# Attention and expert kernel: queries and keys with four tokens to a lane, ten output tiles, and a new order

## The chip, the cores and the metric

The kernel runs on one core of one Trainium2 chip. The metric is the time of one execution on the device, in microseconds (us). A core has five engines that run side by side: TensorE (PE), VectorE (DVE), ScalarE (ACT), GpSimd (POOL) and SyncE (SP), which here only issues transfers; 16 DMA engines move the data between the memory of the chip (HBM) and the 128 lanes of the core's own memory (SBUF). PE writes into PSUM, which has eight banks of 2 KB per lane.

## The reference

Two layers of attention, one behind the other, on 4 sequences of 768 tokens.

```python
# layer 1: q, k, v are (4, 8, 768, 64) in float32; n_global = 8, n_local = 96
scores = scale * np.matmul(q, k.transpose(0, 1, 3, 2))
is_global = pos[None, :] < int(n_global)
is_local = (rel >= 0) & (rel < int(n_local))
keep = is_global | is_local
...
a = np.exp(scores)
a = a / (np.sum(a, axis=-1, keepdims=True) + 1e-09)
x = np.matmul(a, v)
# layer 2: 4 experts of head size 64 on x as (4, 768, 512); the best 2 of 4 by x @ w_gate
for e in range(E):
    q = x @ wq[e]
    k = x @ wk[e]
    v = x @ wv[e]
    scores = scale * (q @ k.transpose(0, 2, 1))
    ...
    ye = a @ v @ wo[e]
```

In layer 1 a token sees the 8 first tokens of its sequence and the 96 last ones before it, with a bias that falls with the distance at a slope of its head's own. In layer 2 it sees all tokens before it. The output is (4, 768, 512) in float32, the weighted sum of the two best experts.

## The kernel before

**Units.** The work is cut into 24 units of 128 tokens, six to a sequence. A unit u runs through a fixed set of steps, each with a short name, and each step is a few instructions on one engine:

- `ldq`, `ldk`, `ldv` load q, k and v (SP). `cq`, `ck`, `cv` cast them to 16 bits (POOL; in the first unit ACT and DVE). `tq` and `tk` transpose on PE, `eq` and `ek` copy the result out of PSUM into qT and kT (DVE).
- `s0` and `s1` are the scores of the heads 0 to 3 and 4 to 7 (PE, line 650), `x0` and `x1` their exponentials (ACT, line 654), `m0` and `m1` the product with the mask and bias table M (DVE, line 659), `z` the product with v (PE, lines 670 and 672), `r` and `n` the division by the sum (DVE, lines 678 and 679).
- `kp` and `vp` put the 8 global tokens' keys and values over the first 8 places of a unit's k and v once that unit has used its own, so that the next unit finds them beside the local ones: `kp` is a copy on POOL, and `vp` (line 686) a transfer of 8 KB from one place of SBUF to another, issued by SP when `z` of its unit is done; `z` of the next unit waits for it. `kg` and `vg` keep the 8 tokens of each sequence in KG and VG.
- `tx` and `ex` transpose the result of layer 1; `pq` (line 704) and `pv` (line 710) are the projections of layer 2, `eqk` and `ev` take them out of PSUM, `xr`, `mx`, `wr`, `zi` make the experts' weights; `s2`, `x2` (line 746), `af` (line 754), `y2` (line 766), `rz`, `cw`, `n2` are the second attention, over all units of the sequence so far.
- `tz`, `ez`, `po` (line 789), `eo` and `so` (line 798) are the output projection, its copy out of PSUM and the store of 256 KB.

**Order.** All of this is written out by hand in one table, `ORDER`: every entry is a step and a unit (`s0-2`), with a star where the second of two allowed engines takes it, and the PSUM banks it uses behind a colon. `+14` behind the bank puts 14 idle matmuls of a zero tile ahead of the step (line 381, "busy"). Every engine, and SP, works through its own steps in the order of the table. The table starts with constants: `M-0-0` to `M-1-1` build the mask table on ACT, `w-q`, `w-k`, `w-v`, `w-o` cast the weights, `warm` is 24 idle matmuls.

**Tiles of q and k.** Before the change, units go in pairs: a block is 256 tokens of all 8 heads, one load for q and one for k, 512 KB each. A lane holds two neighbouring tokens, so a packet is 2 x 64 x 4 = 512 B. There are twelve blocks and three buffers of each kind (`RB = 3`). The transposed columns of a unit then stand in the order (token parity, lane); the mask table is built in that order, and `perm` puts it right in `tx`. `ek` is one copy of 128x1024 16-bit elements, since for k the two tokens of a lane are transposed as one 32-bit word, which leaves the keys in their own order.

**Other buffers.** Most tiles have four copies (`R = 4`), the output tile o_sb among them: `eo` of a unit waits for `so` of the unit four before it.

Of the kernel before, what the change touches and what calls it, by code (L numbers as in the profile page):

```python
# [16 lines left out]
P = 128  # L17
# [5 lines left out]
V1one* ldk-0 nil iota warm:1 ld-g ident ldk-2 perm dg ldq-0 ck0-0 ldv-0 ones d mask ident32 ldq-2 d0  # L23
d1 ck1-2 w-g M-1-0 ck1-0 ck0-2 ld-k M-0-1 tk-2:4+10 tk-0:3 cq0-0 ek-0 ldq-4 cq1-0 cv-0 M-0-0 ek-2
tq-0:6+16 vg-0 M-1-1 eq-0 ldv-1 s0-0:45+14 s1-0:67 cq0-2 x1-0 kg-0 x0-0 cq1-2 kp-0 ld-q m0-0
s1-1:01+25 m1-0 s0-1:23 x1-1 w-k* tq-2:6 z-0:45 x0-1 m1-1 vp-0 eq-2 cq0-4 r-0 kp-1 cq1-4 n-0 ldk-4
tq-4:2+19 V2one cv-1 s0-2:45 eq-4 s1-2:01 kp-2 x1-2 m0-1 ldv-2 ld-v w-q* z-1:23+10 x0-2 s1-3:01 r-1
s0-3:67 m1-2 vp-1 tx-0:5 x0-3 n-1 ck0-4 ex-0 x1-3 tx-1:2 kp-3 pq-0:6 ck1-4 ex-1 ldq-6 m0-2 pq-1:1
eqk-0* cv-2 m1-3 tk-4:7 ldv-3 eqk-1* ldk-6 w-v* z-2:45 ek-4 s20-0:01 s1-4:67 x20-0 m0-3 pv-0:3 vp-2
x1-4 r-2 af-0 s0-4:01 n-2 kp-4 x0-4 cq1-6 s0-5:67 s20-1:45 cq0-6 ldk-8 x0-5 tx-2:1 m0-4 tq-6:2 cv-3  # L30
ex-2 xr-0 x20-1 s1-5:67 m0-5 pq-2:0 ldv-4 mx-0 x1-5 wr-0 ck1-6 eq-6 z-3:45 ck0-6 vp-3 pv-2:6 r-3
zi-0 n-3 tk-6:1 xr-2 eqk-2* ldq-8 m1-4 ev-2 s20-2:45 ck0-8 ev-0* pv-1:7 x20-2 ek-6 tx-3:3 ck1-8
ldv-6 mx-2 s0-6:01 ldq-10 wr-2 cv-4 s1-6:45 ex-3 tk-8:6 x1-6 m1-5 z-4:23 ev-1 af-1 x0-6 ek-8 pv-3:5
vp-4 xr-1 af-2 r-4 s21-2:01 mx-1 xr-3 zi-2 pq-3:6 n-4 x21-2 cq0-8 mx-3 wr-1 kg-6 m1-6 ld-o y2-0:7
eqk-3* y2-1:0 kp-6 m0-6 tx-4:1 ev-3 cv-6 wr-3 s1-7:23 ex-4 s0-7:45 x1-7 cq1-8 rz-0 rz-1 y2-2:6 cw-0
vg-6 zi-1 tq-8:1 n2-0 ldv-5 x0-7 cw-1 pq-4:2 ldk-10 cq1-10 eq-8 kp-7 rz-2 tz-0:7 m1-7 eqk-4*
s21-3:45 cw-2 x21-3 ez-0 ldq-12 s20-3:23 n2-2 w-o* n2-1 tz-2:1 z-6:67 x20-3 ez-2 vp-6 r-6 s0-8:01
n-6 x0-8 cv-5 s1-8:23 s20-4:45 m0-7 po-0:7 x1-8 po-2:0 cq0-10 eo-0* tz-1:6 ldk-12 kp-8 x20-4 ez-1
z-5:23 ck0-10 eo-2* tx-6:6 ck1-10 po-1:7 ex-6 s1-9:01 r-5 eo-1 m1-8 pq-6:6 ldv-7 x1-9 n-5 cq0-12
ldk-14 s0-9:45 m0-8 eqk-6* s21-4:23 tq-10:0 kp-9 x21-4 m1-9 tx-5:6 ldv-8 tk-10:1 cq1-12 ex-5 x0-9  # L40
af-3 s20-6:23 ek-10 tq-12:7 ck1-12 pq-5:6 x20-6 ldq-14 eq-10 ck0-12 eq-12 s22-4:01 eqk-5* s1-10:23
cv-7 tk-12:7 x22-4 m0-9 z-7:45 x1-10 ek-12 ck1-14 s21-5:01 vp-7 r-7 x21-5 kg-12 pv-4:2 n-7 ck0-14
ldk-16 pv-6:3 cv-8 s0-10:45 xr-6 mx-6 xr-4 mx-4 ev-4 zi-3 tx-7:1 kp-10 x0-10 y2-3:7 ex-7 tk-14:6
m1-10 ldv-9 ev-6 s20-5:45 ldq-18 cq0-14 wr-4 s1-11:01 rz-3 x20-5 pq-7:2 cw-3 af-4 n2-3 ek-14 cq1-14
tz-3:7 z-8:45 eqk-7* wr-6 ez-3 tq-14:3 x1-11 ck0-16 vp-8 zi-4 r-8 n-8 s0-12:67 af-6 pv-7:2 x0-12
ldq-16 eq-14 ck1-16 s1-12:01 s0-11:45 x1-12 s22-5:67 m1-11 tk-16:3 ev-7 xr-7 x0-11 cv-9 y2-4:0 mx-7
wr-7 ek-16 so-1 af-5 pv-5:1 so-0 zi-6 tx-8:4 m0-10 ev-5 z-9:23 xr-5 x22-5 cq1-18 ex-8 po-3:5 r-9
kp-12 pv-8:4 n-9 cq0-18 eo-3 so-2 s0-13:67 mx-5 rz-4 cq1-16 s1-13:23 wr-5 x0-13 pq-8:5 cw-4 ldv-10
cq0-16 zi-5 n2-4 m0-11 x1-13 vp-9 tq-16:0 m1-12 tq-18:1 eqk-8* eq-16 tz-4:7 ldk-18 s20-7:23 ez-4
tx-9:5 m0-12 x20-7 y2-5:6 eq-18 ldv-12 y2-6:7 xr-8 mx-8 ev-8 ex-9 s21-8:01 s20-8:23 cv-10 ldv-11  # L50
rz-6 x21-8 rz-5 pq-9:5 wr-8 cw-6 kp-13 x20-8 n2-6 cw-5 z-10:01 zi-7 m1-13 eqk-9* po-4:7 vp-10 af-8
r-10 n2-5 s20-9:23 eo-4 n-10 s0-14:45 af-7 pv-9:6 x20-9 ck1-18 ldk-20 tz-5:0 tx-10:7 y2-8:1 ez-5
xr-9 cv-12 x0-14 zi-8 mx-9 y2-7:0 ex-10 s21-9:23 rz-8 ev-9* ldv-13 pq-10:7 cw-8 x21-9 rz-7 m0-14
so-4 cv-11 pv-10:5 n2-8 eqk-10* tz-6:4 cw-7 wr-9 s1-14:23 xr-10 ev-10 mx-10 ez-6 z-11:67 kp-14 x1-14
n2-7 ck0-18 ldv-14 wr-10 s21-10:01 zi-10 s20-10:45 vg-12 r-11 x21-10 n-11 tk-18:3 ldq-20 po-6:2
ek-18 x20-10 cv-13 po-5:7 eo-6* tz-8:6 ck0-20 z-12:01 eo-5 tx-11:3 vp-12 ez-8 s0-15:45 af-9 ex-11
s1-15:67 x0-15 r-12 zi-9 pq-11:3 af-10 ldq-22 n-12 kp-15 x1-15 m0-15 tx-12:4 y2-9:2 ex-12 eqk-11*
s0-16:01 rz-9 m0-13 s1-16:45 so-5 x0-16 s22-10:67 pq-12:3 so-3 cq0-20 cw-9 x22-10 cq1-20 n2-9
z-13:01 eqk-12* m0-16 tz-7:2 tq-20:6 x1-16 ldk-22 r-13 ez-7 n-13 cq0-22 s20-12:23 vp-13 x20-12
s20-11:45 eq-20 ck1-20 s21-11:01 tx-13:2 m1-14 x21-11 po-8:3 ldv-16 cv-14 tz-9:7 po-7:6 eo-8* x20-11  # L60
kp-16 s22-11:01 cq1-22 ez-9 tk-20:3 ex-13 x22-11 m1-16 s1-17:45 ldv-15 tq-22:7 ek-20 so-8 ck0-22
eo-7 z-14:01 x1-17 m1-15 s0-17:23 vp-14 pq-13:6 kg-18 eq-22 ck1-22 x0-17 r-14 m1-17 po-9:4 eqk-13*
tk-22:5 so-7 n-14 eo-9 cv-15 s1-18:67 s20-13:23 x1-18 s0-18:01 ldv-17 af-12 tx-14:4 ek-22 x0-18
z-15:67 cv-16 x20-13 ex-14 pv-11:0 vp-15 kp-18 r-15 m0-17 s0-19:45 xr-11 so-9 s1-19:23 m0-18 x0-19
pq-14:1 kp-19 n-15 af-11 x1-19 mx-11 ldv-18 m1-18 tx-15:6 af-13 wr-11 z-16:45 ex-15 eqk-14* cv-17
ev-11* s1-20:23 vp-16 r-16 s0-20:67 n-16 x1-20 y2-10:1 ldv-19 m0-19 s20-14:45 x0-20 s21-14:23 rz-10
pq-15:0 zi-11 so-6 cw-10 n2-10 x20-14 cv-18 z-17:67 m0-20 eqk-15* pv-12:5 kp-20 r-17 vg-18 n-17
x21-14 tx-16:4 cv-19 s1-21:01 ev-12 ex-16 s0-21:23 xr-12 x1-21 mx-12 af-14 z-18:67 wr-12 pq-16:4
vp-18 m1-19 x0-21 ldv-23 kp-21 r-18 y2-11:5 n-18 ldv-20 eqk-16* zi-12 s0-22:01 rz-11 s21-15:23
ldv-22 cw-11 x0-22 y2-12:4 n2-11 pv-14:7 rz-12 tx-18:6 cw-12 x21-15 tz-10:5 mx-14 n2-12 pv-13:1  # L70
ez-10 tx-17:0 ldv-21 ex-18 ev-13 s20-15:45 ex-17 s21-16:23 xr-14 xr-13 x20-15 m0-22 tz-11:6 pq-17:0
mx-13 ez-11 x21-16 wr-14 af-15 po-11:5 wr-13 eqk-17 po-10:6 cv-20 eo-11 ev-14* s22-16:01 s20-16:23
eo-10 m1-21 s1-22:45 x22-16 kp-22 so-10 z-19:67 zi-13 m1-20 x20-16 y2-13:0 vp-19 pq-18:1 r-19 cv-21
n-19 x1-22 so-11 af-16 rz-13 s21-17:23 eqk-18 s0-23:67 x21-17 pv-16:5 m0-21 tz-12:4 pv-15:1 x0-23
cw-13 ez-12 z-20:23 n2-13 mx-15 zi-14 tz-13:0 vp-20 xr-15 cv-23 r-20 ev-16 s22-17:67 n-20 ev-15
po-12:4 xr-16 cv-22 x22-17 mx-16 ez-13 tx-19:2 wr-16 y2-14:3 wr-15 eo-12 ex-19 s1-23:67 s20-17:01
rz-14 x1-23 cw-14 so-12 y2-15:2 zi-16 m0-23 z-21:45 zi-15 x20-17 n2-14 po-13:6 vp-21 m1-22 pv-18:7
eo-13 r-21 rz-15 pq-19:0 n-21 so-13 mx-18 cw-15 tx-20:1 n2-15 eqk-19* pv-19:6 xr-18 s20-18:45
s20-19:23 wr-18 x20-18 ev-19* y2-16:0 ex-20 x20-19 af-18 zi-18 z-22:45 rz-16 cw-16 pq-20:1 af-17
vp-22 mx-19 xr-19 ev-18 n2-16 r-22 af-19 wr-19 tz-14:7 n-22 tz-15:3 eqk-20* pv-17:6 ez-14 y2-19:2  # L80
zi-19 ev-17 m1-23 tx-21:1 xr-17 y2-18:4 tx-22:7 po-14:5 rz-18 mx-17 ex-21 y2-17:0 rz-19 wr-17 eo-14
cw-18 ex-22 pq-21:1 so-14 n2-18 rz-17 cw-19 ez-15 z-23:45 n2-19 eqk-21* s21-20:23 s20-20:67 r-23
# [267 lines left out]
def kernel(  # L350
# [56 lines left out]

    HP = P // 2  # L410
    ident = const.tile([P, P], FH, name="ident")
    ident32 = const.tile([P, P], F32, name="ident32")
    perm = const.tile([P, P], FH, name="perm")
# [463 lines left out]
```

## Time and profile before

| what | us |
| --- | --- |
| three runs | 145.97, 147.48, 148.12 |
| median of the runs | 147.48 |
| profiled execution, its own time | 146.46 |
| span of it, first to last instruction | 144.7 |
| mean granted TensorE clock in it | 0.991 |

The span is the stretch between the first and the last instruction of the program in the profiled execution; the execution's own time has 1.8 us more around it. The costliest groups of instructions by what they do, from the groups by line with shapes kept apart:

| step | engine | instructions | mean ns of one | busy us |
| --- | --- | --- | --- | --- |
| x0, x1 (128x1024) | ACT | 40 | 1031 | 39.9 |
| x2 (128x1024) | ACT | 36 | 1034 | 36.2 |
| m0, m1 (128x1024) | DVE | 40 | 777 | 30.9 |
| n | DVE | 24 | 688 | 16.5 |
| ck | POOL | 22 | 815 | 17.5 |
| cv | POOL | 24 | 694 | 16.6 |
| cq | POOL | 22 | 654 | 14.2 |
| eqk | ACT | 22 | 590 | 13.0 |
| ek | DVE | 12 | 685 | 8.1 |
| eq | DVE | 12 | 684 | 8.1 |
| eo | ACT / DVE | 16 / 8 | 598 / 687 | 9.4 / 5.5 |

Loads of q take 6.5 us in the median from issue to landing, of k 4.3, of v 3.4, stores 4.7. The DMA packets are 24,576 of 512 B (q and k), 24,576 of 256 B (v), and a few thousand of 1 and 2 KB (weights and stores).

How to read such rows: in a list of waits, a row is "engine line <- who ended the wait: us in total, times, longest". In the timeline a row is start, duration, engine, line, operation, output and input with shapes, count, and in brackets the idle time of that engine before it and what ended it. In the chain of waits a row is start, duration, and what the chain ran through.

### The profile page before, as it was taken

The numbers are of one execution on the slowest core, as the hardware profiler recorded it, in microseconds if no ns is written. First come the engines' busy times: TensorE is split into PE (matmuls) and PEld (weight loads), VectorE is DVE, ScalarE is ACT, GpSimd is POOL, SyncE is SP. The second block draws the span as 40 slices with busy tenths as digits, with TensorE's granted clock in tenths as the row PEclk, the third lists the DMA queues.
The fourth block names the chain that finished last, engine by engine and source line by source line (L and its number), as shares of the span: only waits on it lengthen the run. The fifth ranks groups of instructions, "written<-read, shape, count | busy, mean of one in ns | idle before, by whom it ended". The sixth has DMA issues, their size and how long they took to land.

```text
span 144.7 us, 5721 instructions
## 1 busy us (share of the span) xinstructions
PE 132.1 (91%) x2316; PEld 104.5 (72%) x2316; DVE 119.2 (82%) x375; ACT 116.1 (80%) x193; POOL 79.0 (55%) x142
## 2 busy tenths in 40 slices
PE   6999788899889999999999999999999999999960
PEld 2378667677765887869787957798969789886720
DVE  0265879699988997899889999899999989887970
ACT  3098567888698988988998999999999976699740
POOL 5258767698759898890659477666044304012300
PEclk9999999999999999999999999999999999999996
DMA  2999999986999997999599698565494120121463
GB/s 67 303 266 313 223 252 283 228 190 177 282 273 238 277 226 195 198 333 262 120 240 263 155 337 188 146 156 143 114 185 152 50 106 7 72 77 72 149 250 126
DMA packets 55726, 27.85 MB, mean 192 GB/s; under 512 B 26096, under 2 KB 52368, under 8 KB 55696
## 3 DMA queue, kind: packets, MB, share of 16 engines
q1 hardware_dynamic: 55696, 27.45, 73.0%
q8 instruction: 19, 0.31, 0.9%
q14 instruction: 11, 0.09, 0.2%
HBM read 20.98 MB, written 6.29 MB: 188 GB/s over the span
## 4 chain that ended last, share of the span: by engine, by line
PE 60%; ACT 11%; DMA 10%; DVE 7%; issue 4%; POOL 4%; SPq 0%; ACTq 0%; DVEq 0%; POOLq 0%
PE banks L704 11%; DMA V<-VG 7%; PE banks L650 6%; PE banks L710 6%; PE banks L509 5%; PE banks L742 5%; PE banks L766 5%; ACT A L654 4%; ACT A L746 4%; PE banks L789 4%; PE banks L381 4%; DMA rawqk<-in_k_dram 3%; PE banks L670 3%; PE banks L611 3%; PE banks L694 3%
## 5 line engine op out<-in xcount | busy, mean ns | idle before, releaser
L654 ACT ACTIVATE A<-banks 128x1024 f16<-128x1024 f32 (+1 forms) x48 | 44.4, 959 | 5.5 <-PE banks L650 5.2
L746 ACT ACTIVATE A<-banks 128x1024 f16<-128x1024 f32 (+1 forms) x48 | 42.9, 927 | 2.8 <-PE banks L742 2.4
L659 DVE TENSOR_TENSOR A<-A,M 128x1024 f16<-128x1024 f16 (+1 forms) x48 | 34.8, 736 | 3.4 <-ACT A L654 3.3
L754 POOL TENSOR_SCALAR_AFFINE_SELECT A<-A 128x512 f16<-128x512 f16 x24 | 16.1, 681 | 26.7 <-ACT A L746 21.9
L704 PE MATMUL banks<-xT,wqk 128*128 128x128 f16 x384 | 25.3, 219 | 0.1
L704 PEld LDWEIGHTS <-wqk 128*128 128x128 f16 x384 | 22.0, 98 | 1.8
L400 POOL CAST V<-rawv 128x512 f16<-128x512 f32 x24 | 16.6, 694 | 9.4 <-DMA rawv<-in_v_dram 7.3
L400 POOL CAST k<-rawqk 128x512 f16<-128x512 f32 x22 | 17.5, 815 | 2.7 <-DMA rawqk<-in_k_dram 2.4
L650 PE MATMUL banks<-qT,kT 64*128 64x128 f16 x352 | 16.8, 218 | 1.3 <-POOL kT L400 0.5
L400 POOL CAST q<-rawqk 128x512 f16<-128x512 f32 x22 | 14.2, 654 | 6.6 <-DMA rawqk<-in_q_dram 6.3
L742 PE MATMUL banks<-QK 64*128 64x128 f16 x336 | 16.0, 217 | 1.5 <-ACT A L654 0.6
L679 DVE TENSOR_TENSOR x<-banks,rall 128x512 f16<-128x512 f32 x24 | 16.5, 688 | 0.5
L400 ACT CAST QK<-banks 128x512 f16<-128x512 f32 x22 | 13.0, 590 | 4.1 <-PE banks L704 3.9
L742 PEld LDWEIGHTS <-QK 64*128 64x128 f16 x336 | 10.4, 94 | 6.6 <-issue 4.4
L710 PE MATMUL banks<-wvg,xT 128*128 128x264 f16 x96 | 14.5, 276 | 0.4 <-DVE xT L400 0.2
L650 PEld LDWEIGHTS <-kT 64*128 64x128 f16 x352 | 10.7, 94 | 5.5 <-issue 2.6
L670 PE MATMUL banks<-V,A 128*128 128x65 f16 x192 | 14.3, 193 | 0.3
L789 PE MATMUL banks<-wo,zT 128*128 128x512 f16 x48 | 13.7, 380 | 0.1
L766 PE MATMUL banks<-V,A 128*128 128x65 f16 x336 | 13.4, 193 | 0.0
L670 PEld LDWEIGHTS <-A 128*128 128x128 f16 x192 | 12.1, 97 | 1.4 <-issue 0.5
L672 PE MATMUL banks<-V,A 128*128 128x65 f16 x160 | 12.3, 193 | 0.3 <-DMA V<-VG 0.2
L766 PEld LDWEIGHTS <-A 128*128 128x128 f16 x336 | 11.9, 97 | 0.9
(72 smaller groups left out, 229.5 us busy)
## 6 DMA issues: line engine op xcount, KB each, us to landing
rawqk<-in_k_dram SPq DMA_DIRECT2D x12, 512.0 KB, 4.3
rawqk<-in_q_dram SPq DMA_DIRECT2D x12, 512.0 KB, 6.5
rawv<-in_v_dram SPq DMA_DIRECT2D x24, 256.0 KB, 3.4
out_dram<-o_sb SPq DMA_DIRECT2D x24, 256.0 KB, 4.7
w<-in_moe_wk_dram SPq DMA_DIRECT2D x1, 512.0 KB
w<-in_moe_wq_dram SPq DMA_DIRECT2D x1, 512.0 KB
w<-in_moe_wv_dram SPq DMA_DIRECT2D x1, 512.0 KB
wo<-in_moe_wo_dram SPq DMA_DIRECT2D x1, 512.0 KB
```

The costliest lines, as they stand in the source:

```text
L400: act.copy(o, i) if e == "ACT" else (dve if e == "DVE" else pool).tensor_copy(o, i)
L650: mm(sc[:, par, pr, prev * P:(prev + 1) * P], lhsT=share(kT, u - prev)[L, p, :], rhs=share(qT, u)[L, p, :], start=True, stop=True)
L654: act.activation(A1[(2 * u + hf) % (2 * R)][:, :, :, 0:w], T.pop(("s", u, hf))[:, :, :, 0:w], func=Exp, scale=scale1)
L659: eng[e].tensor_tensor(a, a, M[:, hf, :, :, :] if ri else M0[:, hf, :, :, :], op=Alu.mult)
L670: mm(z[:, h // 4, h % 4, :], lhsT=a[:, 0:P], rhs=V1[i][:, h, 0:DV], start=True, stop=not ri)
L679: add("n", lambda e: dve.tensor_tensor(x16[i][:, :].rearrange("p (f h d) -> p f h d", f=2, d=Dh), T.pop(("z", u))[:, :, :, 0:Dh], r1.unsqu ...
L704: mm(ps[:, j, :], lhsT=wqk[:, ko, j, :], rhs=xT[i][:, ko, :], start=(ko == 0), stop=(ko == nko - 1))
L710: mm(ps[:, :], lhsT=xT[i][:, ko, :], rhs=wvg[:, ko, :], start=(ko == 0), stop=(ko == nko - 1))
L742: mm(sc[:, par, n, :], lhsT=QK2[b % 2][L, ki, 2 + p2, :], rhs=QK2[b % 2][L, ri, p2, :], start=True, stop=True)
L746: act.activation(A2[i][:, :, 4 * ch:4 * ch + m, :], T.pop(("s2", u, ch))[:, :, 0:m, :], func=Exp, scale=scale2)
L766: mm(z[:, ex, :], lhsT=A2[i][:, ex % 2, n, :], rhs=V2[b % 2][:, ki, ex, 0:DV], start=(j == 0), stop=(j == len(mine) - 1))
L789: mm(ps[:, :], lhsT=zT[i][:, p2, :], rhs=wo[:, p2, :], start=(p2 == 0), stop=(p2 == E // 2 - 1))
```

## The change

Five things change at once.

1. A lane holds four neighbouring tokens of q and k, so a packet is 1 KB. The six units of a sequence are no longer three pairs: the first block is units 0 and 1 with all heads, and the other four units make two blocks, one with the heads 0 to 3 and one with 4 to 7. There are again twelve blocks of 512 KB for q and for k. The first block has only 64 lanes' worth of tokens (256/4), so its heads 0 to 3 are loaded into lanes 0 to 63 and its heads 4 to 7 into lanes 64 to 127, by two loads of 256 KB. The transposed tiles get five buffers (`RT = 5`). The steps are now called `ldq-6`, `cqa-6`, `cqb-6`, `tq-6` for a first block and `ldq0-8`, `cq0a-8`, `tq0-8` and so on (`0` and `1` for the halves of the heads) for the others.
2. The keys need a reordering on the way out of PSUM, so `ek` is two copies with pairs of elements as the innermost run. `kp` is two copies for the units 2 to 4 of a sequence. Mask table and `perm` go by four instead of two.
3. The output tile has ten copies instead of four.
4. In the last two units (22 and 23) `y2` is cut: `y1` takes the first eight entries as soon as their exponentials are there, `y2` the rest. The last two outputs are copied and stored in halves (`eo1`, `so1`).
5. The order table is new, with 1048 entries instead of 1042. Its idle matmuls are 90 instead of 94. `w-q` is on DVE instead of POOL; of `eqk` four instead of two are on DVE, of `ev` nine instead of eight, of `eo` five instead of eight.

```diff
-    RB = 3
-    rawqk = ring(RB, [P, 2, H, 2, Dh], F32, "rawqk")
+    RB, RT = 3, 5
+    rawqk = ring(RB, [P, 2, 8 * P], F32, "rawqk")
...
-    o_sb = ring(R, [P, Dm], F32, "o_sb")
+    RO = 10
+    o_sb = ring(RO, [P, Dm], F32, "o_sb")
...
+            def load(n, src):
+                def fn(e):
+                    for f in range(2) if hf is None else [None]:
+                        lanes, hs, toks = ((slice(0, P), slice(4 * hf, 4 * hf + 4), slice(2 * P, S)) if f is None else
+                                           (slice(f * P // 2, (f + 1) * P // 2), slice(4 * f, 4 * f + 4), slice(0, 2 * P)))
+                        nc.sync.dma_start(raw[n][lanes].rearrange("p h j d -> p h (j d)"),
+                                          src[b, hs, toks, :].rearrange("h (p j) d -> p h (j d)", j=4))
+                return fn
...
-            add("ek", lambda e: copy(e, kT[bl % RB][:, :, :, :].rearrange("l h a p -> l h (a p)"),
-                                     T.pop(("tk", u))[:, :, :].bitcast(FH)), {"DVE": 0.6}, ["tk"] + before(3))
+            def ek(e):
+                ps = T.pop(("tk" + gn, u)).bitcast(FH).rearrange("l (h t p j) -> l h p t j", h=2, t=2, j=2)
+                o = kT[nb % RT][:, :].rearrange("l (h p t j) -> l h p t j", h=2, t=2, j=2)
+                for p in range(2):
+                    copy(e, o[:, p, :, :, :], ps[:, p, :, :, :])
...
+        if ri == 0:
+            group("", 3 * b, None)
+        elif ri == 2:
+            for hf in range(2):
+                group(str(hf), 3 * b + 1 + hf, hf)
...
+        cut = 4 * (n_ch - 1) if u >= NU - 2 else 0
...
+        if cut:
+            add("y1", y2(0, cut), {"PE": 0.03 * 2 * cut}, ["af"] + [f"x2{ch}" for ch in range(n_ch - 1)] +
+                [("ev", b * n_rt + ki) for ki in range(ri)] + ["ev"], kind="b", until=[["rz", "cw", "n2"]])
+            add("y2", y2(cut, 2 * (ri + 1)), {"PE": 0.03 * 2 * (2 * (ri + 1) - cut)}, ["y1", f"x2{n_ch - 1}"])
...
+        parts = 2 if u >= NU - 2 else 1
...
+            add("so" + nm, lambda e, cs=cs: nc.sync.dma_start(out[b, rows, cs], o_sb[u % RO][:, cs]),
+                {"DMA": 0.92 if parts == 1 else 0.5}, ["eo" + nm])
```

The two tables begin like this on PE and on SP (the other engines' steps left out):

```
before, PE: warm tk-2+10 tk-0 tq-0+16 s0-0+14 s1-0 s1-1+25 s0-1 tq-2 z-0 tq-4+19 s0-2 s1-2 z-1+10 s1-3 s0-3 tx-0
after, PE:  warm tk-0 tk1-2 tq-0 s0-0+16 s1-0 s1-1+21 s0-1 tk0-2 tq0-2+15 z-0+6 tq1-2+9 tx-0 s0-2 s1-2+5 s1-3+8 s0-3 s0-4 s1-4 z-1
before, SP: ldk-0 ld-g ldk-2 ldq-0 ldv-0 ldq-2 ld-k ldq-4 ldv-1 ld-q vp-0 ldk-4 ldv-2 ld-v vp-1 ldq-6 ldv-3 ldk-6 vp-2 ldk-8 ldv-4 vp-3
after, SP:  ldk1-2 ldk-0 ldq-0 ldk0-2 ldv-0 ldq0-2 ldq1-2 ld-g ldv-1 ld-q ld-k vp-0 ld-v ldv-2 ldq-6 vp-1 ldk-6 ldv-3 ldk0-8 vp-2 ldk1-8 ldv-4 ldq0-8 vp-3
```

and end like this on PE:

```
before: s21-23 pv-22 po-16 pv-21 po-18 s20-23 s22-23 y2-21 y2-22 y2-20 po-19 tz-21 y2-23 tz-22 po-21 po-22 tz-20 tz-23 po-20 po-23 total
after:  s21-23 po-18 y2-21 po-19 po-16 y1-22 s20-23 y2-22 s22-23 tz-21 pv-23 y2-20 po-21 tz-22 y1-23 tz-20 y2-23 po-22 po-20 tz-23 po-23 total
```

## The prediction

> **What bounds the kernel now.** I read the page's busy shares and slices first, then the windows of 5 us, then the waits of ACT and DVE stage by stage, then the chain of waits and the timeline of the last 10 us.
>
> ```profile
> PE 132.1 (91%) x2316; PEld 104.5 (72%) x2316; DVE 119.2 (82%) x375; ACT 116.1 (80%) x193; POOL 79.0 (55%) x142
> DVE  0265879699988997899889999899999989887970
> DMA  2999999986999997999599698565494120121463
> 15.00:20.00 5.00, 3.71 (x72) 3.36 (x73) 4.01 (x10) 2.69 (x4) 3.30 (x6) 1.00 0.87 230
> 20.00:25.00 5.00, 4.31 (x78) 3.76 (x78) 4.20 (x7) 4.08 (x6) 4.12 (x6) 1.00 1.08 271
> 85.00:90.00 5.00, 4.88 (x78) 3.49 (x75) 4.96 (x8) 4.83 (x6) 4.15 (x7) 1.00 1.05 245
> 120.00:125.00 5.00, 5.00 (x110) 4.65 (x109) 4.43 (x22) 2.69 (x8) 1.03 (x2) 1.00 0.16 57
> ```
>
> The window rows give busy us of PE, PEld, DVE, ACT, POOL, then the granted clock (1.00: it is out of the argument), DMA share and GB/s. Three stages differ. From 45 to 110 us DVE and ACT are both near 95% (4.96 and 4.83 of 5): bound by their work, and an added DVE instruction counts almost whole. From 110 to 130 PE never pauses (5.00) while ACT falls to 2.69. In the first 45 us nobody is full, and the DMA engines are, until about 30 us.
>
> ```profile
> ACT A L654 <- PE banks L650: 4.4, 5, 2.3
> DVE A L659 <- ACT A L654: 3.3, 3, 1.7
> 19.06 1.94 ACT L654 ACTIVATE A<-banks 128x1024 f16<-128x1024 f32 x2 [2.31 <-PE banks L650]
> 26.48 2.85 ACT L654 ACTIVATE A<-banks 128x1024 f16<-128x1024 f32 x3
> 20.62 4.45 DMA V<-VG
> ```
>
> The two waits are those of 14 to 45 us: ACT loses 4.4 us waiting for scores, and DVE 3.3 us waiting for ACT. The exponentials of unit 2 start at 19.06 behind PE, which has tq-4 and 19 fillers ahead of s0-2; those of unit 4 start only at 26.48, since k of units 4 and 5 is a block of its own, issued at 16.71 behind vp-0 and landed at 21.0. The last row is from the chain: a copy of 8 KB (vp) takes 4.45 us, because it stands in the DMA queue behind loads.
>
> ```profile
> 134.09 1.62 PE L766 MATMUL banks<-V,A 128*128 128x65 f16 x48
> 134.18 1.98 ACT L746 ACTIVATE A<-banks 128x1024 f16<-128x1024 f32 x2
> 136.09 0.93 PE L766 MATMUL banks<-V,A 128*128 128x65 f16 x24
> 139.98 0.69 DVE L400 COPY o_sb<-banks 128x512 f32<-128x512 f32 x1 [0.44 <-ACT o_sb L400]
> ```
>
> The last exponential ends at 136.16; the last output copy at 140.67; its store, issued at 140.70, closes the span of 144.7. These 8.5 us are latency, not work.
>
> **Part 1: 1 KB packets and half lanes.** Bytes are unchanged; q and k go from 24,576 packets of 512 B to 12,288 of 1 KB. In the packet records 512 B take 32.1 ns and 1 KB (the weights) 55.6, so 16 engines save (24,576 x 32.1 - 12,288 x 55.6)/16 = 6.6 us of work in the whole run; only what lies before 30 us can show. Where 512 B packets run alone (5 to 8 us) 290 GB/s flow, with 1 KB about 325 (11 to 13, and 16 to 17 us). Until q of the first block 1.57 MB pass in both tables (k1-2, k-0, q-0 against k-0, k-2, q-0): 5.4 us against 4.8, -0.6 us. But k-0 and q-0 (1.05 MB) now come as two loads each on 64 lanes. No row has 64 lanes; the nearest is V<-VG on 8, whose packets of 1,056 B take 65.6 ns, 18% over the 1 KB ones: 3.2 us x 0.18 = +0.6. I take 0 for the head; ends -0.6 and, at half the rate of 1 KB, 3.2 - 0.6 = +2.6. ACT then still runs two casts of q (1.12 us) and eight factors (2.13) before x0-0, which began at 12.98, as before; the factor M-1-0, moved behind x1-0, delays x1-1 by 1.07 us at most, inside its wait for PE. SP issues eight more loads (0.4 us each): nothing waits for SP there but vp, which waits for z anyway.
>
> [...]
>
> **Part 2: blocks of four units by heads.** Unit 2 now needs k0-2, q0-2, and its second half k1-2, q1-2: 3.4 MB instead of 2.36 MB must be in, so s0-2 comes no earlier than 18.4 us. After that units 2 to 5 have all their scores without another load: PE's order reads s0-2 s1-2 s1-3 s0-3 s0-4 s1-4, and the waits of ACT between 20 and 30 us go. Of 4.4 us I take 2.0: the 2.31 before unit 2 stays, the later ones go; ends 0 and -4.4. What is late next is z, tied by vp: 1.25 MB stand between vp-0 and vp-1 in both tables, and between vp-1 and vp-2 too. The cast of wq goes from POOL (1.29 us a weight) to DVE, between m0-2 and m1-2: DVE has 3.2 us of idle time from 19 to 45 us to hide it; +0.5, ends 0 and +1.2.
>
> **Part 3: ek in two pieces.** One copy of 128x1024 f16 takes 685 ns, one of 128x512 f16 (xT) 417: 12 x (2 x 417 - 685) = +1.8 us on DVE, of which some 85% lie in full stages: +1.5. The read goes in pairs of elements, which no row shows; if it falls to the speed of an f32 copy (687 ns for 512), 12 x (2 x 687 - 685) = +8.3. Lower end +0.9 (instructions overlap by 75 ns: 0.34 from start to start). The row of xT is nearest, as PSUM, f16 and length agree.
>
> **Part 4: the table in the middle.** Two eqk, one ev more and three eo fewer on DVE: 2 x 692 + 413 - 3 x 687 = -0.3; ACT gets the reverse, +0.2. Counting PE's matmuls ahead of each pq, the tables differ by under 2 us throughout, so the solid PE stage neither moves nor shrinks: 0, ends -1 and +1. kp in two pieces adds 12 x 0.2 us to POOL, which is idle for 45% of the span. If POOL's cover fails (it has 4.85 of 5 from 30 to 35), the same 2.4 us would come in at kp, before the next unit's scores. Ten output tiles let stores wait without holding eo; the waits at eo are for po (ACT 2.7, DVE 0.6) and for ACT's eo (0.4), none for a store: 0.
>
> **Part 5: the tail.** Behind s22-23 PE has 72 matmuls of y2 (30 ns), 5 po (0.43), 4 tz (0.11) now: 4.7 us; then 36, 4, 4 and one pv (0.45): 3.7, so -1.0. The last copy in halves on ACT and DVE: 0.69 to about 0.42, -0.3. The last store lands after 4.0 us; one that ran alone took 2.0, so half the bytes give -0.7. Against it 36 matmuls of y2 and a po (1.5 us) stand ahead of s20-23 and s22-23 now; ACT was full there (133.7 to 136.2), I charge 0.5. Sum -1.5, ends 0 and -2.5.
>
> **Sum.** 0 - 2.0 + 0.5 + 1.5 - 0.3 - 1.5 = -1.8 us. The profiled execution took 146.46 (span 144.7 and 1.8 around it); the median of the runs is 147.48. From 147.0 between them: 145.2.
>
> **Rivals.**
> Paid in full: half lanes cost nothing (-0.6), ACT's regained time reaches DVE whole (-3.3, its wait), ek at the overlapped price (+1.0), the rest as above: -0.6 - 3.3 + 0.5 + 1.0 - 0.3 - 2.0 = -4.7, so 142.3. For it: the waits are there, in a stage that feeds all others. Against it: DVE is full from 45 us on and has more to do.
> Slower, by half lanes: if a half-lane load runs at half rate, k-0 and q-0 add 2.6, and k-6 and q-6, which stand ahead of vp-1 and vp-2, 1.6 each on the chain through z: 145.2 + 5.8 = 151.0. It decides from about 80 ns a packet on half lanes: (80/55.6 - 1) x 3.2 - 0.6 = 0.8 at the head and 0.7 for each of the other two, 2.2 in all, and the gain is gone. For it: vp has 4.45 us on the chain already. Against: the 65.6 ns of V<-VG.
> Slower, by ek at 8.3: 145.2 + 6.8 = 152.0. For it: DVE is full. Against: both sides stay two-byte runs.
> No effect (packets were hidden anyway, and what the tail gains is lost ahead of it): 147.0.
>
> **How the numbers follow.** Forecast 0.42 (its own range 143.8 to 146.8), paid in full 0.33, half lanes 0.16, ek 0.05, no effect 0.04. A difference under about 2% can't be told from none here; 2% under 147.48 is 144.5. Faster: 0.30 of the second and 0.08 of the first, 0.38. Slower: 0.14 + 0.05 and 0.01, 0.20. Within: 0.42. The range 142.0 to 149.2 reaches over the second case and into the third's lower sizes; under 142 I leave 0.07, above 0.13.
>
> **What would show it.** Packets: mean of 1 KB packets of q and k, apart for the first blocks, near 56 to 66 ns; from 80 up the half lanes decide. Part 2: ACT's wait for scores between 14 and 45 us at 2.4 or less, unit 4's first exponential before 24 us. Part 3: the copies of kT at 24 x 417 ns. Tail: under 7.5 us from the last exponential's end to the span's end. I am wrong if DVE's idle time before 45 us doesn't shrink, or if the middle stages, not head and tail, carry the difference.

## The result, and the profile after

The kernel after takes 152.67 us (median of 152.22, 153.11, 154.62 and 151.81), where the kernel before took 146.92 beside it: 1.037 times as long, with an interval of 1.025 to 1.049. It is slower, and outside the range of the prediction (142.0 to 149.2); nearest is its rival "slower, by half lanes" (151.0). Ratios, here and below, are to runs of the kernel before on the same chip and leave disturbed runs out, which the medians don't. The profiled execution took 152.22 us, 5.8 more than that of before, with a span of 150.4.

The page's busy times and three of its rows of 40 slices:

```profile
PE 135.5 (90%) x2312; PEld 107.4 (71%) x2312; DVE 118.5 (79%) x388; ACT 115.9 (77%) x195; POOL 79.6 (53%) x153
DVE  1143498779998938889999899979889989977960
PEclk9995999999999996999999999999999999999996
DMA  2999939999869997989939946476900141222862
```

DVE has no more work than before (118.5 against 119.2 us), so its work in sum is not what costs 5.8 us. The idle places of DVE are the first slices and slice 15 (53 to 56 us), and in the clock row two slices, 4 and 16, stand at 5 and 6 tenths; before had no such slice ahead of its end. The windows show the same (busy us of PE, PEld, DVE, ACT, POOL, then the granted clock, DMA share, GB/s):

```profile
5.00:10.00 5.00, 4.61 (x24) 2.24 (x22) 1.48 (x4) 0.12 (x1) 1.98 (x4) 1.00 1.13 222
10.00:15.00 5.00, 3.89 (x40) 3.33 (x41) 1.43 (x4) 4.05 (x12) 2.68 (x6) 0.66 1.14 314
50.00:55.00 5.00, 2.57 (x46) 1.99 (x41) 3.34 (x6) 3.88 (x4) 2.37 (x4) 1.00 1.16 209
55.00:60.00 5.00, 5.00 (x68) 4.46 (x68) 3.85 (x8) 2.33 (x4) 4.96 (x8) 0.66 0.81 230
125.00:130.00 5.00, 5.00 (x115) 4.47 (x113) 4.73 (x22) 2.72 (x6) 1.94 (x3) 1.00 0.17 59
```

From 5 to 10 and from 50 to 55 us the DMA engines are full (a share of 1.13 and 1.16) and move only 222 and 209 GB/s; from 10 to 15, just as full, 314. The slow windows are those in which loads of 64 lanes run. The solid stage of PE (125 to 130: 5.00, ACT 2.72) is the one that before had from 120 to 125, only later.

The waits between 14 and 45 us, in total, times and the longest:

```profile
ACT A L709 <- PE banks L705: 5.3, 4, 3.1
DVE kT L401 <- PE banks L649: 3.7, 1, 3.7
DVE A L714 <- ACT A L709: 0.3, 1, 0.3
```

ACT's wait for scores has grown from 4.4 to 5.3 us. DVE's wait for ACT has gone (3.3 to 0.3), but DVE now waits as long for the transposes of k0-2, which the new table puts ahead of unit 0's products. Three transfers in the chain of waits are longer than any in the chain of before, whose longest is a load of k of 5.05 us (start, us):

```profile
3.55 6.57 DMA rawqk<-in_q_dram
26.71 5.77 DMA rawqk<-in_k_dram
46.94 8.00 DMA V<-VG
```

The first is the load of q-0: ACT casts it from 10.20 us on, in the kernel before from 9.61. The second is the upper half of k-6. The third is a vp that stands behind q-12 and k-12, 8.00 us for 8 KB, where the vp in the chain of before took 4.45 and 5.04 us. The end of the span:

```profile
140.19 1.94 ACT L807 ACTIVATE A<-banks 128x1024 f16<-128x1024 f32 x2 [0.17 <-PE banks L803]
145.74 0.37 ACT L401 COPY o_sb<-banks 128x256 f32<-128x256 f32 x1 [0.85 <-PE banks L866]
146.15 0.42 DVE L401 COPY o_sb<-banks 128x256 f32<-128x256 f32 x1 [0.76 <-ACT o_sb L401]
```

From the last exponential's end (142.13) to the span's end (150.4) pass 8.3 us, before 8.5; the two halves of the last copy run one behind the other.

### The profile page after: what moved, and what is told of

Same layout as the page of the kernel before. It is cut to its first block, busy times and chain, and to the rows that moved or that the text cites. A ratio compares the mean times of both kernels' runs of the same rounds, so it can differ in the third digit from the quotient of the medians.

```text
span 150.4 us, 5766 instructions
## 1 busy us (share of the span) xinstructions
PE 135.5 (90%) x2312; PEld 107.4 (71%) x2312; DVE 118.5 (79%) x388; ACT 115.9 (77%) x195; POOL 79.6 (53%) x153
## 4 chain that ended last, share of the span: by engine, by line
PE 57%; DMA 15%; ACT 13%; DVE 5%; issue 3%; SPq 2%; POOL 2%; ACTq 0%; DVEq 0%; POOLq 0%
PE banks L765 10%; DMA V<-VG 7%; PE banks L705 6%; PE banks L836 6%; ACT A L807 6%; PE banks L803 6%; PE banks L771 6%; PE banks L866 5%; DMA rawqk<-in_q_dram 4%; DMA rawqk<-in_k_dram 4%; ACT A L709 4%; PE banks L642 3%; PE banks L725 3%; PE banks L382 3%; PE banks L649 3%; PE banks L727 3%
## 5 line engine op out<-in xcount | busy, mean ns | idle before, releaser
L815 POOL TENSOR_SCALAR_AFFINE_SELECT A<-A 128x512 f16<-128x512 f16 x24 | 16.6, 698 | 23.6 <-ACT A L807 18.3
L765 PE MATMUL banks<-xT,wqk 128*128 128x128 f16 x384 | 25.9, 221 | 0.2
L401 POOL CAST k<-rawqk 128x512 f16<-128x512 f32 x22 | 16.7, 790 | 10.0 <-DMA rawqk<-in_k_dram 10.0
L401 POOL COPY kT<-KG 128x16 f16<-128x16 f16 (+1 forms) x32 | 9.1, 298 | 19.2 <-PE banks L705 19.1
L705 PE MATMUL banks<-qT,kT 64*128 64x128 f16 x352 | 17.4, 222 | 1.4 <-ACT A L709 0.7
L401 POOL CAST V<-rawv 128x512 f16<-128x512 f32 x24 | 16.0, 667 | 4.7 <-DMA rawv<-in_v_dram 4.5
L401 ACT CAST QK<-banks 128x512 f16<-128x512 f32 x20 | 12.0, 602 | 5.3 <-PE banks L765 5.3
L725 PE MATMUL banks<-V,A 128*128 128x65 f16 x192 | 14.7, 193 | 1.5 <-POOL V L401 1.0
L725 PEld LDWEIGHTS <-A 128*128 128x128 f16 x192 | 12.2, 97 | 5.2 <-issue 3.2
L727 PE MATMUL banks<-V,A 128*128 128x65 f16 x160 | 12.3, 193 | 2.9 <-DMA V<-VG 2.8
L401 ACT COPY o_sb<-banks 128x512 f32<-128x512 f32 (+1 forms) x21 | 11.8, 574 | 3.1 <-PE banks L866 3.0
L836 PE MATMUL banks<-V,A 128*128 128x65 f16 x336 | 14.1, 193 | 0.0
```

Of the source, the lines that this page charges most:

```text
L401: act.copy(o, i) if e == "ACT" else (dve if e == "DVE" else pool).tensor_copy(o, i)
L705: mm(sc[:, par, pr, prev * P:(prev + 1) * P], lhsT=share(kT, u - prev, hf)[L, pr, :], rhs=share(qT, u, hf)[L, pr, :], start=True, stop=True)
L725: mm(z[:, h // 4, h % 4, :], lhsT=a[:, 0:P], rhs=V1[i][:, h, 0:DV], start=True, stop=not ri)
L727: mm(z[:, h // 4, h % 4, :], lhsT=a[:, P:2 * P], rhs=V1[(u - 1) % R][:, h, 0:DV], start=False, stop=True)
L765: mm(ps[:, j, :], lhsT=wqk[:, ko, j, :], rhs=xT[i][:, ko, :], start=(ko == 0), stop=(ko == nko - 1))
L836: mm(z[:, ex, :], lhsT=A2[i][:, ex % 2, n, :], rhs=V2[b % 2][:, ki, ex, 0:DV], start=(lo == 0 and n == (ex // 2 if cut else mine[0][0]) an ...
```

## The experiments

The theory after these readings: loads of 64 lanes are slow and put everything behind them off, at the start and at each sequence again. Its rivals: the order of the table (ek0-2 ahead of unit 0's products), the half clock after PE's pauses, ek in two pieces. The kernel after has a ratio of 1.037 [1.025, 1.049]; times in us per part are differences of ratios, with the interval in brackets where it matters. In the runs with odd and even lanes the line numbers are 9 to 11 higher than in the kernel after.

**Half lanes on the kernel before.**

```diff
-    rq[:, n, ...], src[b, :, ri * P:(ri + 2) * P, :]
+    for f in range(2) if ri == 0 else [None]:
+        rq[f * P // 2:(f + 1) * P // 2, n, ...], src[b, :, f * P:(f + 1) * P, :]
```

> The kernel before, with one edit: q and k of the first block of every sequence come as two loads of 64 lanes each; packets stay at 512 B, the order and the output stay the same. Theory half lanes: these loads run at the 207 to 228 GB/s that the kernel after shows from 5 to 9 us, so k-0 and q-0 (1.05 MB) take about 4.8 us where the kernel before took 3.6 (290 GB/s); q of the first block lands 1 to 1.5 us later than 9.17, the first n (17.4) starts 1 to 2 us later, and the time is 1.5 to 3 us above that of before. Rival, order of the table (DVE has ek0-2 ahead of the first m in the kernel after, not here): q lands at most 0.5 us later and the time stays within 1 us of before.

152.84 us, ratio 1.040 [1.033, 1.046]: as large a loss as that of the whole change, on the old kernel, by that edit alone, and more than the 1.5 to 3 us expected. Window 5 to 9 us of the kernel before, of this run, of the kernel after:

```profile
5.00:9.00 4.00, 4.00 (x22) 1.89 (x21) 2.76 (x8) 1.44 (x5) 2.57 (x6) 1.00 1.23 280
```
```profile
5.00:9.00 4.00, 4.00 (x24) 1.93 (x23) 1.99 (x8) 0.66 (x3) 1.89 (x6) 1.00 1.18 234
```
```profile
5.00:9.00 4.00, 3.89 (x19) 1.76 (x18) 0.79 (x2) 0.12 (x1) 1.98 (x4) 1.00 1.13 217
```

The last number is the rate: 280, 234 and 217 GB/s, with the engines equally full. In this run the window also holds k-2, which has all 128 lanes: from 6 to 7.5 us, in its time, 302 GB/s flow, and from 8 to 9, with q-0 on half the lanes, 189, both in packets of 512 B. ACT casts q at 11.01 us, 1.4 later than before. That its loss is only 0.9 us at the first n, 3.1 at unit 3 and 5 from unit 7 on says that the start is the smaller part here.

**Other lanes on the kernel after.** The two loads go to even and odd lanes; the same rows of HBM, bytes and packets.

```diff
-    (slice(f * P // 2, (f + 1) * P // 2), slice(4 * f, 4 * f + 4), slice(0, 2 * P))
+    (slice(f, P, 2), slice(4 * f, 4 * f + 4), slice(0, 2 * P))
...
+    pool.tensor_copy(odd.rearrange("c (f p) -> c f p", f=2), ident.rearrange("c (p f) -> c f p", f=2))
...
-    nc.tensor.transpose(to[:, p, :, j, :], q_[:, j, 2 * p:2 * p + 2, :], ident)
+    nc.tensor.transpose(to[:, p, :, j, :], q_[:, j, 2 * p:2 * p + 2, :], odd if hf is None else ident)
```

> The kernel after, with the two loads of a first block on even and on odd lanes in place of the lower and the upper 64, and the transposes of first blocks against an identity with its columns in that order; bytes, packets and output are the same. Theory half lanes: the 1 KB packets from 5 to 9 us fall from 82 to 87 ns to below 60, q of the first block lands at 9.0 to 9.4 in place of 10.15, the copy vp that took 8.00 us at 47 to 55 falls below 6, and the time falls by 2 to 4 us against the kernel after (to 148.5 to 150.5). Rival, order of the table: the time falls by 1 us at most and n of unit 0 still starts after 19 us (before: 17.4). Rival, number of lanes (64 lanes are slow, whichever): packets stay above 75 ns and the time does not change.

145.95 us, ratio 0.994 [0.990, 0.998], where the kernel after has 1.037: all that was lost comes back, and a little more, where 2 to 4 us were expected. The same window:

```profile
5.00:9.00 4.00, 4.00 (x19) 1.89 (x18) 1.47 (x2) 0.46 (x2) 2.68 (x6) 1.00 1.06 333
```

In the packet records the 1 KB packets of 5 to 9 us take 51.5 ns, where those of the kernel after took 84.0 (45 to 54 us: 52.5 against 98.5). Spread over the whole width 64 lanes are as fast here as 128 (51.5 ns and 343 GB/s from 11 to 13 us of this run, where only loads of 128 lanes flow). ACT casts q at 8.65 us, no slice is at half clock (mean 0.997), and the longest vp on the chain is 4.56 us in place of 8.00:

```profile
26.39 4.56 DMA V<-VG
```

**Order and clock.**

```diff
-x1-1 ek0-2 cq0a-2 kp-1 tq0-2:3+15 m1-0 x0-1 ld-q m0-0 ld-k cq1b-2 eq0-2 z-0:67+6 cq1a-2 r-0 n-0 vp-0
+x1-1 m1-0 m0-0 z-0:67+6 r-0 n-0 ek0-2 cq0a-2 kp-1 tq0-2:3+15 x0-1 ld-q ld-k cq1b-2 eq0-2 cq1a-2 vp-0
```

> The kernel after, with unit 0's m1-0, m0-0, z-0, r-0 and n-0 moved ahead of ek0-2 and tq0-2 in the table. Theory order: the first m runs at about 15.5 instead of 17.79, n of unit 0 starts 1.5 to 2.3 us earlier than 19.8, and the time falls by 1.5 to 2.5 us against the kernel after. Theory half lanes: unit 0 gains, but unit 1 and 2 still wait for their loads, n of unit 1 moves by under 0.7 us from 25.6, and so does the time.

152.75 us, 1.026 [1.018, 1.035], with runs from 149.69 to 154.41: not told apart from the kernel after.

```diff
-tq-0:5
+tq-0:5+40
```

> The kernel after, with 40 idle matmuls on PE ahead of the transposes of the first q, where PE waits for that load. Theory clock (PE's pause at 9.7 to 10.9 us costs a stretch of 3.4 us at half clock from 11.6): the granted clock of 10 to 15 us is 1.00 in place of 0.66, the first scores of unit 1 come 1 to 1.5 us earlier, and the time falls by 1 to 1.5 us. Theory half lanes: what follows waits for loads, not for PE; the clock is restored and the time falls by under 0.5 us.

152.51 us, 1.037 [1.031, 1.044]. The windows of this run:

```profile
10.00:15.00 5.00, 5.00 (x91) 4.78 (x90) 2.06 (x5) 3.99 (x12) 2.72 (x6) 1.00 1.14 312
55.00:60.00 5.00, 3.29 (x59) 2.71 (x55) 3.17 (x8) 2.11 (x5) 4.45 (x7) 1.00 0.77 221
```

The clock is full in both places, n of unit 1 comes 0.8 us earlier, and by unit 2 that is gone; from 55 to 60 PE, no longer slowed, idles for 1.7 us instead. The idle matmuls need not be what kept the clock: the profiles of three runs below without them, with the first loads on half lanes too (middle sequences only, two issuers, m first once more; mean clock 0.997, 0.998 and 0.998, where the kernel after has 0.970), also show 1.00 from 10 to 15 us, with pauses of PE of 1.1 to 1.4 us at 10 us, where the kernel after had 1.2. The run with two issuers, with a mean clock of 0.998, still takes 153.16 us. The half clock was not the cause of the loss.

**Which sequence pays.** Odd and even lanes in sequence 0 only (`if b in (0,)`), then in 1 and 2 only.

> The kernel after, with odd and even lanes in sequence 0 only; the first blocks of the other three keep lower and upper halves. Theory head (the loss arises in the first 10 us and is then carried along): n of unit 1 starts by 23 us in place of 25.6, the lead is kept, and the time is 146 to 147.5. Rival, later sequences (k-6, q-6, k-12 and q-12 stand ahead of the vp copies that the chain through z waits for): n of unit 1 gains the same 3 us, but n of unit 8 (65.2) gains less than 1.5, and the time is 150.5 to 152.

> The kernel after, with odd and even lanes in sequences 1 and 2 only; k-0 and q-0 keep lower and upper halves. Theory head: n of unit 1 stays at 25.6 and the time within 1.2 us of the kernel after, 151.4 to 152.7. Rival, later sequences: n of unit 1 stays at 25.6, but vp at 47 to 55 us takes under 6 us in place of 8.00, n of unit 8 starts by 62 in place of 65.2, and the time is 148 to 149.5.

149.56 us, 1.018 [1.011, 1.025], and 150.3 us, 1.027 [1.022, 1.033]. Neither theory holds alone. When n of some units starts (us):

```
unit     before  after  half on before  odd/even  first only  middle only
0          17.4   19.8            18.3      16.7        17.4         18.6
1          21.3   25.6            22.5      22.5        23.2         24.3
3          31.6   36.1            34.7      31.9        33.6         33.9
8          59.1   65.2            63.8      57.5        61.0         59.3
16         96.1  101.6           101.4      94.2        99.0         98.4
23        125.1  129.2           130.1     121.8       126.6         126.0
```

With the first sequence mended 2.4 us are gained by unit 0 and kept; with the middle two mended the gain grows, in a profile of one of its faster runs, from 2.2 at unit 3 to 5.9 at unit 8, of which 3.2 remain. One profile stands behind each column, and they differ by more than the edits: middle only is 1.2 us ahead of the kernel after at unit 0 already, with the same first loads, but a full clock where that has 0.66; as much of the 2.4 us may be of that kind. The lag of the kernel after behind odd/even is 3.1 us at units 0 and 1, 4.2 at unit 3, 7.7 at unit 8, and 7.4 at units 16 and 23: in these two profiles the loss arises at the head and around the first blocks of the second and third sequence, above all at the vp of 8.00 us, and then stays. By the ratios the first sequence alone gives 1.9% (2.7 us [0.7, 4.8]), the middle two 0.9% (1.4 us [-0.6, 3.3]), all four 4.2% (6.2 us [4.4, 8.1]). Whether the parts add up to the whole these intervals don't say.

**The last sequence.** Odd and even lanes in 0, 1 and 2.

> The kernel after, with odd and even lanes in sequences 0, 1 and 2; only k-18 and q-18 keep lower and upper halves. If the loss lies in the first three sequences (where ACT, DVE and PE still wait for loads): the time is that of odd and even lanes everywhere, 145.4 to 146.5. If every sequence pays alike (the loss of 6.2 us in four parts): 147 to 148.

148.61 us, 1.006 [1.000, 1.011]. The median lies above both expectations; half of the runs lie between 146.7 and 148.14, which is nearer to the second, and the ratio's interval lies above that of odd and even lanes everywhere (0.990 to 0.998). That speaks for a share of the last sequence, of 1.6 us [0.7, 2.6]. But runs below with odd and even lanes everywhere and one further edit each have 0.997, 0.998 and 1.001, and the profile can't decide: it is 1.4 us late by n of unit 0 (18.1), long before k-18 is loaded. Whether the last sequence has a share stays open.

**Two issuers.** The second half of k-0 and q-0 from ACT.

```diff
-    nc.sync.dma_start(raw[n][lanes]...
+    (nc.scalar if f == 1 and nb == 0 else nc.sync).dma_start(raw[n][lanes]...
```

> The kernel after, with the second half (lanes 64 to 127) of k-0 and of q-0 issued by ACT instead of SP, so both halves of a load can run at once; all other loads stay. Theory that only one load at a time is slow (each half of the lanes has a path of its own): 300 GB/s or more from 5 to 9 us in place of 207 to 228, q of the first block lands by 9.4 in place of 10.15, n of unit 1 starts 2 us or more earlier than 25.6, and the time falls by 2 to 3 us. Rival (packets of both loads wait for each other in the same 16 engines): at most 245 GB/s, q of the first block after 9.8, and the time within 0.8 us of the kernel after.

153.16 us, 1.045 [1.038, 1.051]:

```profile
5.00:9.00 4.00, 4.00 (x16) 1.65 (x15) 0.69 (x2) 0.10 (x1) 1.97 (x4) 1.00 1.14 210
```

Both halves may now run at once, and the rate is 210 GB/s: no gain, and q is cast at 10.90 us. The rival holds.

**vp on another queue.** On the kernel after, and with odd and even lanes.

```diff
-    add("vp", lambda e: nc.sync.dma_start(V1[i][0:N_G, :, :], VG[b % 2][:, :, :]), ...
+    add("vp", lambda e: nc.scalar.dma_start(V1[i][0:N_G, :, :], VG[b % 2][:, :, :]), ...
```

> The kernel after, with the 8 KB copies vp issued by ACT instead of SP. Theory queue (vp is slow since it stands in SP's queue behind the half-lane loads of the next first block): vp of 47 to 55 us takes under 4 us in place of 8.00, n of unit 8 starts 3 us or more earlier than 65.2, and the time falls by 2.5 to 4 us. Rival (vp's packets share the 16 engines with those loads whatever the queue): it still takes over 6 us and the time falls by less than 1 us, or rises, as ACT now waits for z ahead of its exponentials.

> Odd and even lanes, and vp issued by ACT. Theory queue: the copies vp of 4.56 us at 26.4 and 2.98 us at 86.3 on the chain of the kernel with odd and even lanes fall to about 2 us, and the time to 143 to 144.8. Rival: the time stays within 0.8 us of 145.95, or rises by what ACT loses waiting for z.

160.33 us (155.98 to 163.79) and 156.14 us, 1.064 [1.058, 1.070]: the rise that the rivals allowed for, and a large one. One row of the chain of each, the kernel after's first:

```profile
27.85 5.93 DMA V<-VG
```
```profile
22.39 6.10 DMA V<-VG
```

These are the longest vp on the two chains. At SP the longest were 8.00 us and, with odd and even lanes, 4.56: a queue of its own doesn't bring them to the 2 to 4 us of the theory. SP, no longer held by vp's wait for z, runs ahead with its loads (with odd and even lanes q-6 is issued at 14.90 us in place of 18.39), and ACT waits for z in its place; how much each of these costs was not tried apart.

**The other terms, on the kernel with odd and even lanes.** The last two units whole again (`cut = 0`, `parts = 1`, y1, eo1 and so1 out of the table):

> The kernel with odd and even lanes (145.95), with the last two units whole again: one y2 of 40 and 48 matmuls behind the last exponentials, one copy and one store of each output tile. The prediction's price of the parts, 1.5 us: the time rises by 1 to 2 us, and from the end of the last exponential to the end of the span pass 9.5 to 10.5 us in place of 8.45. Rival (that stretch is 8.45 us with the parts and 8.5 in the kernel before, so they were worth nothing): it stays within 0.5 us of 8.45 and the time within 0.6 of 145.95.

146.76 us, 1.001 [0.998, 1.005] against 0.994: the parts are worth about 1.0 us [0.2, 1.9]. The last exponentials of the run with the parts and of this one:

```profile
132.81 1.94 ACT L816 ACTIVATE A<-banks 128x1024 f16<-128x1024 f32 x2 [0.17 <-PE banks L812]
```
```profile
133.57 2.01 ACT L816 ACTIVATE A<-banks 128x1024 f16<-128x1024 f32 x2
```

With spans of 143.2 and 144.8 this leaves 8.45 and 9.2 us behind them; before had 8.5. So the parts give 0.8 there, and without them the stretch is 0.7 longer than before. The new order of the table's end is the likely reason; it was not tried apart.

```diff
-    for p in range(2):
-        copy(e, o[:, p, :, :, :], ps[:, p, :, :, :])
+    copy(e, kT[nb % RT][:, :], T.pop(("tk" + gn, u)).bitcast(FH))
```

> The kernel with odd and even lanes (145.95), with ek as one copy of 128x1024 f16 in place of two of 128x512, so the keys of a block stay in another order and the scores are those of other pairs than the reference's. The prediction's term (DVE is full from 45 us on, +1.5 us for the two pieces): the copies of kT take 12 x 690 in place of 24 x 415 ns and the time falls by 1 to 1.8 us. Rival, PE carries the end from 85 us on: DVE's busy time falls by 1.7 us and the time by less than 0.4.

146.32 us, 0.998 [0.994, 1.003] against 0.994: no gain, or 0.3 us at most. The copies of kT, two pieces (odd and even lanes) and one:

```profile
L401 DVE COPY kT<-banks x24: 389/414/425, 9.4 to 88.8; 128x512 f16<-128x512 f16 x24
```
```profile
L401 DVE COPY kT<-banks x12: 655/680/692, 9.1 to 89.5; 128x1024 f16<-128x1024 f16 x12
```

The price of the pieces was right, 24 x 414 - 12 x 680 = 1.8 us of DVE, but the end doesn't come earlier when DVE is spared them.

```diff
-    mm(ps[:, :], lhsT=zT[i][:, p2, :], rhs=wo[:, p2, :], ...)
+    for n in range(parts):
+        mm(ps[n][:, cs], lhsT=zT[i][:, p2, :], rhs=wo[:, p2, cs], ...)
```

> Odd and even lanes, with po of the last two units in two banks, one for each half of its columns, so that ACT and DVE copy out of different banks. Theory (the two last copies run one after the other since both read one bank): DVE's last copy starts within 0.1 us of ACT's in place of 0.40 after it, and 8.0 to 8.1 us pass from the last exponential's end to the span's end in place of 8.45; in the time 0.4 us. Rival (DVE's copy waits for something else): it still starts 0.3 us or more after ACT's.

146.37 us, 0.997 [0.993, 1.001], no different in time; but its profile, with a span of 145.8 us, shows the copies apart:

```profile
140.96 0.42 DVE L401 COPY o_sb<-banks 128x256 f32<-128x256 f32 x1
141.17 0.37 ACT L401 COPY o_sb<-banks 128x256 f32<-128x256 f32 x1 [0.86 <-PE banks L877]
```

The copies run side by side: it was the one bank (and the one tile in it) that tied them. From the last exponential's end to the last copy's end pass 4.0 us instead of 4.4, to the span's end 8.25 instead of 8.45.

**Order once more.** In the profile of the first run with m first, one product of 128x512 took 2651 ns. So it was run again, and with odd and even lanes.

> Odd and even lanes, with the order of the run that moved unit 0's m1-0, m0-0, z-0, r-0 and n-0 ahead of ek0-2 and tq0-2. Theory order: with the loads quick, the order is what is left; n of unit 0 starts 1 us or more before 16.7 and the time falls by 0.8 to 1.5 us below 145.95. Rival, DVE's multiply is held up by POOL (one m of 128x512 f16 took 2651 ns in the profile of that run, 411 in the kernel after, while POOL cast q and v without a pause): an m of over 1.5 us shows again, n of unit 0 gains less than 0.5 us and the time stays within 0.6 us of 145.95.

> The kernel after with the same order, a second time, since the first runs of it spread from 149.69 to 154.41. Theory order: n of unit 0 starts by 18.5 and the time is 150 to 151. Rival, the multiply held up by POOL: one of unit 0's two m again takes over 1.5 us, n of unit 0 starts after 19.3 and the time is 151.8 to 152.8.

146.81 us, 0.990 [0.985, 0.995], and 151.44 us, 1.028 [1.025, 1.032]. Unit 0's products in the second of these (min, median, max in ns) and in the kernel after:

```profile
L714 DVE TENSOR_TENSOR A<-A,M x2: 423/1019/1615, 14.6 to 16.1; 128x512 f16<-128x512 f16 x2
```
```profile
L714 DVE TENSOR_TENSOR A<-A,M x2: 411/646/882, 17.8 to 18.6; 128x512 f16<-128x512 f16 x2
```

and what POOL does meanwhile in the second:

```profile
14.16 0.62 POOL L401 COPY VG<-V 8x528 f16<-8x528 f16 x1
14.73 1.17 POOL L401 CAST q<-rawqk 128x512 f16<-128x512 f32 x2
15.85 0.41 POOL L401 COPY kT<-KG 128x32 f16<-128x32 f16 x1
16.22 1.36 POOL L401 CAST q<-rawqk 128x512 f16<-128x512 f32 x2
```

The product that starts at 14.59 ends at 16.2: it lasts over POOL's two casts, and POOL's next small copy then takes 0.41 us, where others of its kind take 0.20. With slow loads n of unit 0 still starts 2.0 us earlier than in the kernel after (17.8), of which 0.6 are left at the last units; but this profile has the full clock, and against the 18.6 of middle only, which has it too, 0.8 are the order's. The time lies between the two expectations. With quick loads n starts at 16.9 in place of 16.7: nothing won there. By the ratios the order of the table has a share of 1.2 us [-0.6, 3.1] with slow loads and 0.6 [-0.3, 1.6] with quick ones, which these runs don't separate from none. This version, odd and even lanes with m first, has the lowest ratio of all, but not by more than the intervals overlap, and within 2% of the kernel before.

## Why the prediction was wrong

**The step that failed** is the cost of the half lanes in part 1: "No row has 64 lanes; the nearest is V<-VG on 8, whose packets of 1,056 B take 65.6 ns, 18% over the 1 KB ones ... I take 0 for the head". Eight packets on 8 lanes say nothing of loads of 256 KB on 64: beside those, at 45 to 54 us of the kernel after, the packets of that same row took 106.6 ns. In place of 65.6 the 1 KB packets took 84.0 ns at the start and 98.5 at 45 to 54 us. The upper end on record, half the rate and +2.6, an estimate without a row behind it, was the nearest: the rate fell to 65% (217 against 333 GB/s), the cast of q comes 1.55 us later than with other lanes (10.20 against 8.65), and the first sequence alone costs 2.7 us [0.7, 4.8]. Part 1 also put the later first blocks at nothing ("only what lies before 30 us can show"); there the lag behind the kernel with odd and even lanes grows from 3.1 to 7.7 us by unit 8. Apart from the half lanes its term was right in sign: with odd and even lanes q of the first block is cast at 8.65 us instead of 9.61, forecast -0.6.

**The rival "slower by half lanes"** had the mechanism and nearly the size: 151.0, from +2.6 at the head and 1.6 each for k-6 and q-6. It named the chain through vp, but the longest vp, 8.00 us, stands behind q-12 and k-12, one sequence later. It got a chance of 0.16. Its own threshold, 80 ns a packet, was passed.

**Part 2** was right in kind: with odd and even lanes ACT waits 2.7 us for scores from 14 to 45 us (forecast 2.4, before 4.4), the six exponentials of units 2 to 4 run back to back from 18.28 us, the first of unit 4 at about 22.0 (18.28 and four of 0.94), and DVE's wait for ACT is gone. But other waits of ACT have grown in the same stretch, for the second layer's scores (L812, before 1.2 us) and for DVE's division (L742, before none):

```profile
ACT A L718 <- PE banks L714: 2.7, 2, 2.4
ACT A L816 <- PE banks L812: 2.3, 1, 2.3
ACT A L718 <- DVE rall L742: 1.3, 1, 1.3
```

ACT is busy for 23.6 us of the 31, before 23.2, and n of units 1 and 3 starts 1.2 and 0.3 us later than before: by unit 3 the 2.0 us that were forecast have not come. In the kernel after the same row starts at 21.37, so unit 4's comes at about 25.1, behind its mark of 24: half lanes covered the gain. The cast of wq took DVE 0.68 us, as charged (0.5).

**Part 3**: the durations held (24 x 414 to 415 ns), the use of DVE's time as the end's didn't: at most 0.3 us instead of +1.5.

**Part 4** was 0, and a difference carried by the middle stages was named as a sign of being wrong. It is there: with odd and even lanes n starts 0.3 us later than before at unit 3, then 1.6 earlier at unit 8, 1.9 at unit 16 and 3.3 at unit 23. Which part of the change wins this was not tried. The other sign came too: DVE's idle time before 45 us grew from 13.2 to 15.7 us in the kernel after (11.7 with odd and even lanes).

**Part 5**: forecast -1.5 against the kernel before, measured 0 (8.45 against 8.5 us). The stretch has 0.4 us since the two halves of a copy wait for each other at one bank, which the text had taken as parallel, and the last store lands 3.8 us after its issue with half the bytes (4.0 before): -0.2 instead of -0.7.

**Sum.** Without the half lanes the forecast was 147.0 - 1.8 = 145.2; the kernel with odd and even lanes takes 0.57% less than before, 0.8 us [0.3, 1.4]. In its profile, which is of its fastest run, n of unit 23 starts 3.3 us earlier than before, but the last exponential ends only 1.4 earlier; between them PE is at 4.7 to 5.0 of 5, so probably its work there takes the rest. In the rival "paid in full" the tail stands with -2.0, where part 5 has -1.5; with that it would be 142.8.

## What to carry to other kernels

Where a load's lanes change, count its rate by the lanes it writes and not by packets: here 64 lanes spread over the whole width moved 333 GB/s and one half of the lanes 217. A row of eight small packets prices no stream of large loads; when no row fits, give the far bound its chance. And mend one part of a change alone before judging the others: here one choice of lanes hid what all the other parts did.

## What the runs showed of the hardware

- Rate by lanes, in packets of 1 KB, the first two with the same rows of HBM: lower and upper 64 lanes 84.0 ns and 217 GB/s, even and odd 64 lanes 51.5 ns and 333 GB/s, all 128 lanes 51.5 ns and 343 GB/s (11 to 13 us of the run with even and odd lanes). With the upper half of the first loads issued by ACT the rate was 210 GB/s.
- A product of 128x512 on DVE, 411 ns at the shortest in the kernel after, took 1615 ns (m first once more) and 2651 ns (the first run with m first) while POOL copied without a pause. In the kernel after the ten casts of v on POOL that ran beside products with M on DVE took 610 to 1067 ns, the other 14 605 to 618.
- In the kernel after the granted clock was 0.50 for 3.4 us from 11.6 and from 56.0 us, after pauses of PE of 1.2 and 1.8 us. Such a pause doesn't decide it alone: after pauses of 1.1 to 1.4 us at the same place it stayed at 1.00 in three other runs. With a mean clock of 0.998 in its profile a run was no faster (153.16 us).
